# Attention with beacon keys into soft-MoE: loads spread over all partitions, the start and the pair loop reordered

## The chip, the cores and the metric

One NeuronCore of a Trainium2 chip runs the whole program. The metric is the device time of one execution in microseconds (us), the median of several runs. The engines are TensorE (PE; its weight loads are PEld), VectorE (DVE), ScalarE (ACT), GpSimd (POOL) and SyncE (SP), which only issues transfers; 16 DMA engines move the data.

## The reference

```python
# q, k, v: (8, 8, 576, 64) = (B, H, S, D); beacon_k, beacon_v: (8, 8, 16, 64); float32
scores = q @ concat(beacon_k, k).T / 8        # 592 keys; causal over the 576, the 16 beacons always seen
x = softmax(scores) @ concat(beacon_v, v)     # -> (4608, 512) tokens
logits = x @ phi                              # 32 slots, 4 per expert, 8 experts
slot_input = softmax(logits, over tokens).T @ x
slot_out[e] = relu(slot_input[e] @ w1[e]) @ w2[e]     # w1: (8, 512, 1024), w2: (8, 1024, 512)
out = softmax(logits, over slots) @ slot_out  # (4608, 512) float32
```

## The kernel before, in words

Everything is ordered by hand: the program runs under a manual schedule, so each engine takes its instructions in the order in which the code emits them, and a tile pool with a number of buffers decides when a new tile must wait for the readers of an old one. PSUM is full: two score tiles of two banks (`ps_sc`, tag sc), one A.V tile of two banks (`ps_av`, tag av), and two single banks (`ps_tr`, tag tr) for transposes and small sums.

**Loads.** SP issues k, q and v (float32, 28.3 MB) by half batches (`load_qk`, four buffers each for k and q) and batches (`load_v`, two buffers; its last 80 rows by `load_vr`). A v tile holds token 4p+t at partition p, shifted so that the 16 beacon rows fill partitions 0 to 3: `load_v` fills all partitions for b > 0 and the beacon rows are laid over partitions 0 to 3 afterwards by `load_bv` (L381), so each of these loads has to wait for the v load of the same tile; for b = 0 it loads partitions 4 to 115 and 116 to 127 (L371). The beacon keys of all heads come in one load over 64 partitions (L669). POOL issues the expert weights (33.5 MB float32, cast to float16 on the way) in 32 pieces of 512 KB (`load_weights`, L448 and L453): one in each pair but the first of a batch, two a pair in the last two batches, and what is left behind the loop. Experts 0 to 4 have room of their own; 5 takes the v buffers (`wv`), 6 and 7 the k and q buffers (`wt`), once these are free. The order of the last six pieces is w2 of experts 5, 6, 7, first halves and then second halves.

**Start** (L699 to L742). PE runs `fill` matmuls (work whose result nobody reads), turns k and q of the first half batch (`transposes`), turns the beacon keys (L710, copied to `bkA` by DVE and from there into `kTs` by POOL, `beacon_keys`), and computes the scores of pairs 0 and 1 with fills between them.

**Pair loop** (L746 to L783), 30 turns, n = 2 to 31; a pair is two heads, four pairs are one batch b. `scores(n, bank)` makes four banks of transposed scores (L514), each followed by an exp on ACT (L519) into `expT` and a causal mask on POOL (`select`, L505). `attend(n-1, hh)` multiplies the probabilities of the pair before by v (L535), `normalize` divides (DVE, L549), `x_transposes(n-3)` turns x (L561), `transposes` turns k or q two half batches ahead (L483, evicted by DVE, L495). One pair is emitted as: scores 0, scores 1, transposes, A.V of head 0, scores 2, x's turn, A.V of head 1, normalize, scores 3. The extras of a batch are put behind this: `dispatch(b-2)` (slot sums) in the first pair, `logits(b-1)` in the third, `combine_T(b-1)` and `perm_v(b+1)` in the fourth. `perm_v` turns the casted v into token order by 16 selecting matmuls into one score tile and both tr banks, and ACT (L407) and DVE (L410) copy it to `vhs`.

**Tail.** The last pair's A.V, logits and slot sums; `first` (relu of slot inputs by w1, L816), `turn`, `second` (by w2, L831); `row_sums(bb)` (L663) make the combine weights' sums for the four quarters of the output, two quarters in a PSUM bank beside the expert output `so`, the other two before and behind `second(1)`. The expert output is scaled (L863), the row factors are inverted (`row_factors`, L841 and L843), and 36 output tiles follow: a matmul (L911), an eviction by ACT or DVE in turn (L916, L918), and 13 stores (L922). `judge` tests on DVE that no sum left the range that the fast path allows; POOL prepares these tests (L884 to L888).

Of the kernel before, what the change touches and what calls it, by code (L numbers as in the profile page):

```python
# [268 lines left out]
def kernel(  # L269
# [39 lines left out]
    bkA = const.tile([P, Nb, B * H], BF, name="bkA")  # L309
# [45 lines left out]
    def load_v(b):  # L355

        t = st["v", b] = stv.tile([P, H, 4, D], FP, name="vstag", tag="v", bufs=2)
        st["r", b] = stv.tile([P, H, D], FP, name="vrem", tag="r", bufs=2)
        if b:
            lo = (b * H * S - Nb) * D
            nc.sync.dma_start(
                out=t[:, :, :, :].rearrange("p h t d -> p h (t d)"),
                in_=v.rearrange("b h s d -> (b h s d)")[lo:lo + H * S * D].rearrange(
                    "(h e) -> h e", h=H)[:, 0:4 * P * D].rearrange("h (p e) -> p h e", p=P))
        else:
            for p0, p1 in ((4, 116), (116, 128)):  # L370
                nc.sync.dma_start(  # L371
                    out=t[p0:p1, :, :, :].rearrange("p h t d -> p h (t d)"),
                    in_=v[b, :, 4 * p0 - Nb:4 * p1 - Nb, :].rearrange(
                        "h (p t) d -> p h (t d)", t=4))
# [4 lines left out]

    def load_bv(b):  # L380
        nc.sync.dma_start(out=st["v", b][0:4, :, :, :].rearrange("p h t d -> p h (t d)"),  # L381
                          in_=beacon_v[b].rearrange("h (p t) d -> p h (t d)", t=4))

    def cast_v(b, c):
# [3 lines left out]
        if c < 2:  # L388
            for hs in (slice(4 * c, 4 * c + 2), slice(4 * c + 2, 4 * c + 4)):
                nc.gpsimd.tensor_copy(  # L390
                    out=st["c", b][:, :, hs, :].rearrange("p t h d -> p h t d"),
                    in_=st["v", b][:, hs, :, :])
        else:
            nc.gpsimd.tensor_copy(out=vhs[b % 2][0:80, 4, :, 0:D], in_=st["r", b][0:80, :, :])

    def perm_v(b):

        ps = ps_sc.tile([P, 2, 512], FP, name="vps", tag="sc")
# [3 lines left out]
        for t in range(4):  # L402
            for c in range(4):
                nc.tensor.matmul(outs[c], sel[32 * c:32 * c + 32, t, :],  # L404
                                 vc[32 * c:32 * c + 32, t, :, :].rearrange("p h d -> p (h d)"),
                                 start=(t == 0), stop=(t == 3))
        nc.scalar.activation(vhs[b % 2][:, 0:2, :, 0:D],  # L407
# [9 lines left out]
    wchunks += [(e, 1, j) for j in range(2) for e in (5, 6, 7)]  # L417
    wtail = {}
# [23 lines left out]
    def load_weights(count):  # L442
        for _ in range(count):
# [7 lines left out]
            else:  # L451
                src = moe_w2[e].rearrange("(p c) d -> p c d", c=NFC)
                nc.gpsimd.dma_start(  # L453
                    out=piece(e, m, j),
                    in_=src[:, 4 * j:4 * j + 4, :].rearrange("p c d -> p (c d)"))
# [3 lines left out]
    def beacon_keys(m):  # L459
        for hh in range(2):  # L460
            c0, c1 = (H * (m // 2) + head(2 * m + u, hh) for u in range(2))
            nc.gpsimd.tensor_copy(  # L462
                out=kTs[m % 2][64 * hh:64 * hh + 64, :, 0:Nb],
                in_=bkA[64 * hh:64 * hh + 64, :, c0:c1 + 1:c1 - c0].rearrange("p n u -> p u n"))

    def transposes(m, which):
# [6 lines left out]
        else:  # L473
            if m:
                beacon_keys(m)
            dst = kTs[m % 2][:, :, Nb:Nb + S]
        for j0, j1 in ((0, 5), (5, NJ)):
            tp = ps_tr.tile([P, j1 - j0, P], BF, name="trps", tag="tr")
# [93 lines left out]
    def logits(b, t0=0, t1=NDC):  # L572
# [12 lines left out]
        if t0 == 0:  # L585
            nc.scalar.activation(dTs[b][:, :, :, :],
                                 lp[:, :, :].unsqueeze(2).broadcast_to([P, NC5, 4, NSL]), AF.Exp)
        else:
            nc.scalar.activation(dTs[b][:, :, 0, :], lp[:, :, :], AF.Exp)
            nc.vector.tensor_copy(  # L590
                out=dTs[b][:, :, 1:4, :],
                in_=dTs[b][:, :, 0:1, :].broadcast_to([P, NC5, 3, NSL]))
# [64 lines left out]
    rsp = {}  # L657

    def row_sums(bb):
        if bb == 0:  # L660
            rsp[0] = ps_av.tile([P, 2, 512], FP, name="rsps", tag="av")
        for j in range(NJ):
            nc.tensor.matmul(rsp[0][:, 1, bb * NJ + j:bb * NJ + j + 1], row_tokens(bb, j),  # L663
                             ones32[:, :], start=True, stop=True)

    with tc.manual_schedule(engines={ET.PE, ET.DVE, ET.Activation, ET.Pool, ET.SP}):
        load_qk(0, 0, first=True)
        bkf = work.tile([P, Nb, D], FP, name="bkf", tag="x")
        nc.sync.dma_start(out=bkf[0:B * H, :, :].rearrange("p n d -> p (n d)"),  # L669
                          in_=beacon_k.rearrange("b h n d -> (b h) (n d)"))  # L670
        load_v(0)
        load_bv(0)
        load_vr(0)
        load_qk(0, 1)
        load_v(1)
        load_qk(1, 0)
        load_bv(1)
        load_vr(1)
        load_qk(1, 1)
# [6 lines left out]
        make_identity(nc, idh)  # L686
        for t in kTs:
# [8 lines left out]
        nc.gpsimd.memset(sel[:, :, :], 0.0)  # L696


        fill(10, False)  # L699
        transposes(0, 0)  # L700
        fill(2, False)
        transposes(0, 1)
        bkh = work.tile([P, Nb, D], BF, name="bkh", tag="vc", bufs=1)
        hi = bkf[0:B * H, :, :].bitcast(BF)[:, :, 1::2]
        nc.scalar.activation(bkh[0:B * H, 8:Nb, :], hi[:, 8:Nb, :], AF.Copy)
        nc.vector.tensor_copy(out=bkh[0:B * H, 0:8, :], in_=hi[:, 0:8, :])
        bkp = ps_tr.tile([P, Nb, B * H], BF, name="bkps", tag="tr")
        for i in range(Nb):
            for hh in range(2):
                nc.tensor.transpose(bkp[64 * hh:64 * hh + 64, i, :], bkh[0:B * H, i, :],  # L710
                                    idb[0:B * H, 0:B * H])
        nc.vector.tensor_copy(out=bkA[:, :, :], in_=bkp[:, :, :])  # L712
        beacon_keys(0)
        fill(5, False)
        for c in range(4):
            for t in range(4):
# [3 lines left out]
                    in_=idh[32 * c:32 * c + 32, 32 * c:32 * c + 32])  # L720

# [3 lines left out]
        for c in range(2):  # L725
            cast_v(0, c)
        for bank in range(2):
            fill(3, False)
# [4 lines left out]
        for bank in range(3):  # L733
            fill(3, False)
            scores(1, bank)
        transposes(1, 0)
        perm_v(0)
        scores(1, 3)
        transposes(1, 1)
        attend(0, 0)  # L740
# [5 lines left out]
        for n in range(2, NPAIR):  # L746
            b, g = divmod(n, NG)
            scores(n, 0)
            scores(n, 1)
            if n // 2 + 1 < 2 * B:  # L750
                transposes(n // 2 + 1, n % 2)
            attend(n - 1, 0)
            scores(n, 2)
            if n >= 3:
                x_transposes(n - 3)
            attend(n - 1, 1)
            if n >= 7 and g == 3:
                combine_T(b - 1)
            normalize(n - 1)
            scores(n, 3)  # L760
            if n == NPAIR - 1:
                x_transposes(n - 2)
            if b and g == 2:
                logits(b - 1)
            if n >= 8 and g == 0:
                dispatch(b - 2)
            if b + 1 < B and g:
                parts = ((0,), (1,), (2,))[g - 1] if b else ((0,), (1, 2))[g - 2]
                for c in parts:
                    cast_v(b + 1, c)  # L770
                if g == 3:
                    perm_v(b + 1)
            if b + 2 < B:
# [3 lines left out]
                if g == 2:  # L777
                    load_bv(b + 2)
# [18 lines left out]
        fill(1)  # L797
# [3 lines left out]
        row_sums(0)  # L801
# [35 lines left out]
        rsv = stat[:, NST:NST + 36]  # L837
        rcf = rc[:, :, :].rearrange("p a j -> p (a j)")

        def row_factors(j0, j1):  # L840
            nc.vector.tensor_scalar(out=rsv[:, j0:j1], in0=rsp[0][:, 1, j0:j1], scalar1=1e-9,  # L841
                                    scalar2=None, op0=AL.add)
# [117 lines left out]
```

## Time and profile before

| what | value |
|---|---|
| median of 3 runs (range) | 203.09 us (202.74 to 204.77) |
| the profiled execution's own time | 203.09 us |
| its span in the profile | 201.4 us |
| PE / DVE / ACT / POOL busy | 163.2 / 132.2 / 133.9 / 113.9 us |
| read from HBM, written to it | 62.69 MB, 9.44 MB |
| TensorE's granted clock, mean | 0.95 |

The profiled execution took as long as the median; 1.69 us of it lie outside of the span. All shares in the profile are of the span. A DMA share of 1 in a stretch means that packets were under way on all 16 DMA engines all the time; a little over 1 is overlap of one packet's end with the next one's start. The weight transfers are counted by the bytes that they write, which is half of what they read.

### The profile page before, as it was taken

To read this page: it belongs to the slowest core of one execution; us is meant where nothing else is said; L and a number is where in the kernel's file an instruction comes from. 1 tells how busy PE (TensorE), PEld (TensorE's weight loads), DVE (VectorE), ACT (ScalarE), POOL (GpSimd) and SP (SyncE) were. 2 spreads that over 40 slices of the span, in tenths; PEclk is the share of its full clock that TensorE was granted. 3 is DMA by queue.
4 is the path that set the end of the run, shared out by engine and by line. 5 is a ranking of instruction groups with operands and counts; after the bars stand their busy time and mean duration, and the time that the engine had idled before them with its cause. 6 is when DMAs were issued, how large, how long until landed. Compare 5 with 4: busy or idle time off the path is not lost.

```text
span 201.4 us, 7361 instructions
## 1 busy us (share of the span) xinstructions
PE 163.2 (81%) x3121; PEld 107.9 (54%) x3121; DVE 132.2 (66%) x275; ACT 133.9 (66%) x172; POOL 113.9 (57%) x263
## 2 busy tenths in 40 slices
PE   6798893889889898988988899898989997966200
PEld 2433661668567476666756667675767753522000
DVE  0352784688987888887887878878837332898300
ACT  2355784689878888889887788987895230774200
POOL 6049186469649757865965786898786000890000
PEclk9999999799999999999999999999999999995855
DMA  6999999999999999999999999999999991499991
GB/s 206 254 244 365 278 361 317 270 370 311 267 271 378 264 261 349 292 275 305 356 232 279 379 273 268 264 219 217 211 216 212 213 202 30 176 410 417 408 405 78
DMA packets 29701, 55.90 MB, mean 278 GB/s; under 512 B 7228, under 2 KB 15644, under 8 KB 29660
## 3 DMA queue, kind: packets, MB, share of 16 engines
q1 hardware_dynamic: 24764, 37.98, 55.4%
q0 software_dynamic: 4608, 16.78, 41.7%
q10 hardware_dynamic: 288, 0.59, 1.0%
q8 instruction: 26, 0.43, 0.8%
q14 instruction: 15, 0.12, 0.2%
HBM read 62.69 MB, written 9.44 MB: 358 GB/s over the span
## 4 chain that ended last, share of the span: by engine, by line
PE 60%; DMA 10%; ACT 9%; DVE 8%; POOL 3%; issue 3%; SPq 0%; ACTq 0%; DVEq 0%; POOLq 0%
PE sc L514 15%; PE av L535 15%; PE trps L483 9%; DMA wt<-in_moe_w_dram 7%; ACT expT L519 5%; PE xtps L561 5%; DVE osb L918 4%; ACT vh L407 4%; PE vpt L404 2%; DMA kstag<-in_k_dram 2%; PE fill L655 2%; PE fps L911 2%; PE lgps L580 2%; PE vps L404 2%; PE sips L619 2%
## 5 line engine op out<-in xcount | busy, mean ns | idle before, releaser
L519 ACT ACTIVATE expT<-sc 128x992 f16<-128x992 f32 (+3 forms) x128 | 104.8, 867 | 20.6 <-PE sc L514 20.0
L505 POOL TENSOR_SCALAR_AFFINE_SELECT expT<-expT 128x224 f16<-128x224 f16 (+3 forms) x128 | 54.9, 439 | 40.1 <-ACT expT L519 39.2
L514 PE MATMUL sc<-qT,kT 64*128 64x80 bf16 (+4 forms) x576 | 43.8, 246 | 10.8 <-ACT expT L519 5.5
L535 PE MATMUL av<-vh,expT 128*128 128x65 f16 (+1 forms) x960 | 40.4, 195 | 0.4 <-DVE x L549 0.2
L535 PEld LDWEIGHTS <-expT 128*128 128x128 f16 (+1 forms) x960 | 33.7, 98 | 4.5 <-POOL expT L505 0.6
L495 DVE COPY kT<-trps 128x640 bf16<-128x640 bf16 (+1 forms) x31 | 22.7, 773 | 19.8 <-PE trps L483 19.3
L514 PEld LDWEIGHTS <-kT 64*128 64x128 bf16 x576 | 17.0, 95 | 28.1 <-issue 22.2
L495 DVE COPY qT<-trps 128x640 bf16<-128x640 bf16 (+1 forms) x30 | 22.0, 774 | 8.2 <-PE trps L483 6.3
L549 DVE TENSOR_TENSOR x<-av,r 128x640 f16<-128x640 f32 x32 | 26.4, 825 | 1.1
L390 POOL CAST vc<-vstag 128x512 f16<-128x512 f32 x32 | 18.6, 611 | 1.8 <-DMA vstag<-in_beacon_v_dram 1.8
L916 ACT ACTIVATE osb<-fps,rc 128x512 f32<-128x512 f32 (+1 forms) x18 | 11.0, 678 | 12.2 <-PE fps L911 10.9
L568 DVE COPY xT<-xtps 128x576 f16<-128x576 f16 x31 | 14.2, 457 | 6.5 <-PE xtps L561 6.5
L561 PE MATMUL xtps<-idh,x 128*128 128x128 f16 (+2 forms) x160 | 14.1, 216 | 1.1 <-issue 1.0
L918 DVE TENSOR_SCALAR osb<-fps,rc 128x512 f32<-128x512 f32 (+1 forms) x19 | 12.8, 731 | 1.3 <-PE fps L911 1.1
L655 PE MATMUL fill<-eT,onesh 128*128 128x512 f16 x35 | 11.4, 453 | 1.7 <-POOL onesh L684 1.5
L407 ACT ACTIVATE vh<-vps 128x1024 f16<-128x1024 f32 x8 | 8.2, 1027 | 6.6 <-PE vpt L404 6.6
L561 PEld LDWEIGHTS <-x 128*128 128x128 f16 (+2 forms) x160 | 9.0, 97 | 6.6 <-issue 6.0
L410 DVE CAST vh<-vpt 128x512 f16<-128x512 f32 x16 | 10.3, 685 | 3.4 <-PE vpt L404 3.4
L911 PE MATMUL fps<-so,eT 128*128 128x512 f16 (+1 forms) x37 | 11.6, 433 | 0.5 <-DVE stat L841 0.3
L462 POOL COPY kT<-bkA 64x32 bf16<-64x32 bf16 x32 | 7.4, 231 | 7.9 <-DVE bkA L712 6.9
L483 PE MATMUL trps<-idb,kstag 128*64 128x128 bf16 x270 | 11.6, 234 | 0.1
L483 PE MATMUL trps<-idb,qstag 128*64 128x128 bf16 x270 | 10.7, 222 | 0.5 <-DVE vh L410 0.4
(98 smaller groups left out, 186.7 us busy)
## 6 DMA issues: line engine op xcount, KB each, us to landing
kstag<-in_k_dram SPq DMA_DIRECT2D x15, 576.0 KB, 9.4
qstag<-in_q_dram SPq DMA_DIRECT2D x15, 576.0 KB, 13.4
out_dram<-osb SPq DMA_DIRECT2D x11, 768.0 KB, 7.6
vstag<-in_v_dram SPq DMA_DIRECT2D x7, 1024.0 KB, 15.3
w1h<-in_moe_w_dram POOLq DMA_DIRECT2D x10, 512.0 KB, 8.6
w2h<-in_moe_w_dram POOLq DMA_DIRECT2D x10, 512.0 KB, 8.5
wt<-in_moe_w_dram POOLq DMA_DIRECT2D x8, 512.0 KB, 12.2
wv<-in_moe_w_dram POOLq DMA_DIRECT2D x4, 512.0 KB, 11.6
```

What stands on the lines that cost most here:

```text
L390: nc.gpsimd.tensor_copy(out=st["c", b][:, :, hs, :].rearrange("p t h d -> p h t d"), in_=st["v", b][:, hs, :, :])
L407: nc.scalar.activation(vhs[b % 2][:, 0:2, :, 0:D], ps[:, :, :].rearrange("p c (h d) -> p c h d", d=D), AF.Copy)
L483: nc.tensor.transpose(tp[lo:hi, j - j0, :], t[:, hh, j, :].bitcast(BF)[:, 1::2], idb[:, :])
L495: nc.vector.tensor_copy(out=do, in_=ti)
L505: nc.gpsimd.affine_select(out=ap, in_=ap, compare_op=AL.is_ge, fill=0.0, base=cbase, pattern=pat, channel_multiplier=-1)
L514: nc.tensor.matmul(sc[:, hh, col:col + qw], kTs[n // 2 % 2][po:po + D, n % 2, c * P:(c + 1) * P], qTs[n // 2][po:po + D, n % 2, q0:q0 + qw ...
L519: nc.scalar.activation(ex[:, :, base:base + w], sc[:, :, 0:w], AF.Exp, scale=scale)
L535: nc.tensor.matmul(av[:, i, :], exps[n % 2][0:KW[c], hh, o:o + P], vhs[b % 2][0:KW[c], c, h, :], start=(c == 0), stop=(c == i))
L549: nc.vector.tensor_tensor(out=xs[b][:, :, head(n, 0):head(n, 1) + 1:head(n, 1) - head(n, 0), :].rearrange("p i h d -> p h i d"), in0=av[:, ...
L561: nc.tensor.transpose(tp[:, QLO[i]:QLO[i] + QW[i]], xs[b][0:QW[i], i, 2 * t:2 * t + 2, :].rearrange("p h d -> p (h d)"), idh[0:QW[i], 0:QW ...
L911: nc.tensor.matmul(f[:, 0:hw], row_tokens(bb, j), so1[:, hw * i:hw * i + hw], start=True, stop=True)
L918: nc.vector.tensor_scalar(out=ou, in0=f[:, 0:hw], scalar1=rc[:, bb, j:j + 1], scalar2=None, op0=AL.mult)
```

## The change

It touches the loads, the start, the order within a pair and the order behind the weights.

- **Loads.** The v load of batch 0 goes over all 128 partitions for heads 1 to 7, as for the other batches; head 0 comes in two loads (partitions 4 to 63, 64 to 127). `load_bv` is gone. The beacon values come with token n at partition n: batch 0's in a load of its own over 16 partitions, all batches' in one load over 128 partitions (`bvf`, 512 KB in pieces of 256 bytes), and `perm_v` adds them by one more matmul, while the rows of `sel` for partitions 0 to 3 are zero. The beacon keys are loaded over 128 partitions. The order on SP is k and q (1, 0) before v (1).
- **Start.** q's turn of the first half batch uses the two banks of the A.V tile. The beacon keys go straight from PSUM to `kTs` by DVE. `sel` is built first. Ten of the fill matmuls are dropped, `perm_v(0)` moves up into pair 1 and uses the A.V tile, and two of the v casts go to DVE.
- **Pair.** All four score banks move ahead of the A.V half that they stood behind, x's turn stands behind the first A.V half, and each batch's extras are one a pair: `perm_v(b)` between scores 0 and 1 of the first pair, `dispatch` in the second, `logits` in the third, `combine_T` in the fourth. The exp of the logits writes one copy, and DVE makes the other three.
- **Tail.** The last weight piece is issued in two halves. `row_sums(0)` and `(1)` have PSUM tiles and factors of their own; `row_sums(2)` and `(3)` are put among the output tiles of quarters 0 and 1, and POOL's test of the sums into `judge`.

```diff
     def load_v(b):
-        if b: ... one load over 128 partitions
-        else:
-            for p0, p1 in ((4, 116), (116, 128)): ... all heads
+        h0 = 0 if b else 1
+        ... one load over 128 partitions of heads h0 to 7
+        if b == 0:
+            nc.gpsimd.memset(t[0:4, 0, :, :], 0.0)
+            for p0, p1 in ((4, 64), (64, 128)): ... head 0
-    def load_bv(b):
-        nc.sync.dma_start(out=st["v", b][0:4, :, :, :].rearrange("p h t d -> p h (t d)"),
-                          in_=beacon_v[b].rearrange("h (p t) d -> p h (t d)", t=4))
     def perm_v(b):
-        ps = ps_sc.tile([P, 2, 512], FP, name="vps", tag="sc")
+        pool, tag = (ps_sc, "sc") if b else (ps_av, "av")
+        ps = pool.tile([P, 2, 512], FP, name="vps", tag=tag)
...
+            if t == 0:
+                lhsT, rhs = (idh[:, b::B], bvh) if b else (idh[0:Nb, 0:Nb], bvh[0:Nb])
+                nc.tensor.matmul(outs[0][0:Nb, :], lhsT, rhs..., start=False, stop=False)
     def load_weights(count):
-                nc.gpsimd.dma_start(out=piece(e, m, j), in_=... 4 columns c)
+                cs = 2 if (e, m, j) == WLAST else 4
+                for c in range(0, 4, cs): ... one load for cs columns
     def logits(b, t0=0, t1=NDC):
-        if t0 == 0:
-            nc.scalar.activation(dTs[b][:, :, :, :],
-                                 lp[:, :, :].unsqueeze(2).broadcast_to([P, NC5, 4, NSL]), AF.Exp)
-        else: ... (as below)
+        nc.scalar.activation(dTs[b][:, :, 0, :], lp[:, :, :], AF.Exp)
+        nc.vector.tensor_copy(out=dTs[b][:, :, 1:4, :],
+            in_=dTs[b][:, :, 0:1, :].broadcast_to([P, NC5, 3, NSL]))
     the pair loop
             scores(n, 0)
+            if b and g == 0:
+                perm_v(b)
             scores(n, 1)
             if n // 2 + 1 < 2 * B:
                 transposes(n // 2 + 1, n % 2)
+            scores(n, 2)
             attend(n - 1, 0)
-            scores(n, 2)
             if n >= 3:
                 x_transposes(n - 3)
+            scores(n, 3)
             attend(n - 1, 1)
-            if n >= 7 and g == 3:
-                combine_T(b - 1)
             normalize(n - 1)
-            scores(n, 3)
+            if b > 1 and g == 1:
+                dispatch(b - 2)
             if b and g == 2:
                 logits(b - 1)
-            if n >= 8 and g == 0:
-                dispatch(b - 2)
+            if b and g == 3:
+                combine_T(b - 1)
...
-                if g == 3:
-                    perm_v(b + 1)
     the tail
-        row_sums(2)
         second(1)
         nc.vector.tensor_scalar(out=so1[:, :], in0=so, scalar1=rd[:, 0:1], ...)
-        row_sums(3)
-        row_factors(2 * NJ, 4 * NJ)
...
                 nc.sync.dma_start(out=outr[bb, :, j0:j1, :], in_=osb[:, 0:j1 - j0, :])
+                if bb in (0, 1) and j0 == 3:
+                    row_sums(bb + 2, ps_g.tile([P, NJ], FP, name="rsps", tag="g"))
```

## The prediction

> **What bounds the kernel now.** I read the DMA rows of the page first, because the kernel reads 62.69 MB.
>
> ```profile
> PEclk9999999799999999999999999999999999995855
> DMA  6999999999999999999999999999999991499991
> GB/s 206 254 244 365 278 361 317 270 370 311 267 271 378 264 261 349 292 275 305 356 232 279 379 273 268 264 219 217 211 216 212 213 202 30 176 410 417 408 405 78
> ```
>
> The 16 DMA engines are full from the second slice to slice 33 (about 166 us), pause for the end of the MLP, and are full again with the stores. Slices with more weights show fewer GB/s, as weights count by what they write: 213 GB/s of weights alone are 426 GB/s read.
>
> The end of the chain of waits says what the pause waits for (start us, us, what).
>
> ```profile
> 154.15 14.88 DMA wt<-in_moe_w_dram
> 169.08 1.04 PE rsps L831 x13
> 170.15 0.76 DVE so L863
> 170.95 0.66 PE rsps L663 x9
> 171.86 0.61 PE fps L911 x3
> ```
>
> The last weight piece lands just before 169.08. Then come the last 16 matmuls of `second`, the scaling, two quarters' row sums, and the first output matmul. But TensorE is nearly late too: in the list of waits this one is only 0.6 us long. So two paths end together at 169: the transfers, and the computing (start, pair loop, MLP). A change must shorten both.
>
> Then I cut the time into stretches, for the DMA share and the rate (last two columns; before them busy us of PE, PEld, DVE, ACT, POOL and the granted clock).
>
> ```profile
> 5.00:13.00 8.00, 6.89 (x87) 3.39 (x85) 4.50 (x20) 2.75 (x4) 0.50 (x2) 1.00 1.16 219
> 13.00:20.00 7.00, 6.23 (x64) 2.48 (x67) 1.46 (x2) 5.09 (x7) 6.16 (x14) 1.00 1.06 364
> 20.00:24.00 4.00, 3.49 (x81) 2.35 (x75) 2.59 (x6) 2.55 (x4) 0.33 (x1) 1.00 0.92 266
> 30.00:36.00 6.00, 2.84 (x44) 1.52 (x46) 2.53 (x6) 3.10 (x5) 3.70 (x8) 0.87 1.09 309
> 86.87:103.57 16.70, 15.58 (x350) 11.26 (x350) 13.96 (x29) 14.46 (x19) 12.09 (x29) 1.00 1.06 301
> 162.00:164.00 2.00, 2.00 (x33) 1.19 (x29) 0.69 (x1) 0.82 (x2) 0.00 (x0) 1.00 1.08 217
> 164.00:166.00 2.00, 2.00 (x34) 1.15 (x36) 0.70 (x2) 0.38 (x1) 0.00 (x0) 1.00 0.92 184
> 166.00:168.00 2.00, 2.00 (x41) 1.15 (x33) 0.44 (x1) 0.00 (x0) 0.00 (x0) 1.00 0.40 82
> ```
>
> Three places waste DMA time. From 5 to 13 us the engines are full (1.16) and move 219 GB/s; the same kind of float32 loads moves 364 right after. From 20 to 24 they are partly empty. From 164 on they run dry one after the other.
>
> SyncE's own waits, and two of the computing engines', complete the picture (total us, times, longest; the third line is of 34.76 to 138.42 us).
>
> ```profile
> SPq L381 <- DMA vstag<-in_v_dram: 39.2, 7, 6.6
> PE sc L514 <- ACT expT L519: 5.5, 10, 0.6
> ACT expT L519 <- PE sc L514: 14.7, 42, 1.5
> ```
>
> The beacon load (L381) overwrites part of the tile that the v load is filling, so SyncE stands, seven times, until v has landed; after the first of these (to 21.05 us) the engines have run empty. In the loop ScalarE is the computing engine nearest to its limit (14.46 of the 16.70 us of a batch) and waits 14.7 us over six batches for scores.
>
> **The transfers, term by term.** What counts is when the last weight piece lands, 168.7 us by its last packet in the trace.
>
> *Loads over all partitions.* In 5 to 13 us lie the beacon keys (64 partitions), batch 0's v (112 and 12), its beacons (4) and its remainder (80). The trace's packet records show the v packets of 1 KB at 65 to 96 ns there and at 46 to 53 in all later v loads, which cover 128 partitions. 219 GB/s for 8 us is 1.75 MB; at 364 GB/s that is 4.8 us. So the most to be won is 3.2 us, the least nothing (if the slowness belongs to the first use and not to the shape). I take 2.6: 896 of the 1020 v packets get the good shape, head 0 and the remainder do not.
>
> *The wait at L381.* 20 to 24 us at 266 GB/s in place of the 349 that I read for 24 to 28 loses 0.95 us. The wait goes with `load_bv`; I take 0.7 off (0 to 1.0). The other six waits cost nothing today, since the share stays at 1.05 or more: weights fill the engines meanwhile.
>
> *Short pieces.* Beacon values now come in 128 + 1024 pieces of 256 bytes. The trace has 5120 such packets (v's remainder): 18 ns median, 24 mean, about 50 in the bad stretch. 1152 x 18 to 24 / 16 engines = 1.3 to 1.7 us: I add 1.5, bounds 0.9 (13 ns, phi's 128-byte packets) and 3.6. They lie in the saturated stretch, so nothing hides them. The Trainium skill (DMA: Bandwidth & Descriptors, "Specifications") asks for 512 bytes at least for the full rate, and so speaks against this part. By it a piece costs no less than one of 512 bytes, an estimate of 23 ns from half of the 1 KB row, 1.7 us in all, and the sum below would be -3.2; the median of 18 ns shows a little less than that.
>
> *Uneven finish.* After 164 us 184, 82 and (168 to 170) 4 GB/s for 2 us each are 0.54 MB; at 217 GB/s all engines would be done at 166.5, 2.2 us before the last one is. Something loads a few engines more than the rest; the eight beacon loads of 4 partitions, 32 packets each, are the only regular small ones. I take 1.6 off, bounds 0 and 2.2. The same page ("Why a DMA increments its semaphore by 16 and not by 1") says that a load takes as many engines as divide its slowest dimension, the lowest-numbered ones: 4 partitions, 4 engines. By it each of these gets an estimated 8 x 8 packets of about 50 ns, 3.2 us, more than the others, which would explain the whole 2.2, and the sum would be -4.0.
>
> Sum: -2.6 - 0.7 + 1.5 - 1.6 = -3.4; the last piece lands at about 165.3.
>
> **The computing.** It must be ready by then, 3.0 us before today's 168.3 (end of the matmuls that needed no wait). *Start:* `bkA` and POOL's copies stand between the beacon turn and the scores (10.41 to 11.73 us); two DVE copies, for which POOL's 0.23 us is the nearest row, save some 0.5. Three fills of 0.75 us between pair 1's scores go, 2.2. `sel`'s 1.96 us on DVE move to where DVE is idle until 7.06. Together -2.5 (bounds 0, -3.2). *Row sums:* `row_sums(2)`, 0.7 us of PE, leaves the place ahead of `second(1)`. That is 3.2, just enough with no gain in the loop at all. *Loop:* with a score bank ahead of each A.V half ScalarE finds work sooner; dT's exp falls from 0.70 to 0.30 us (the rows at L586 and L589), DVE gets 0.31 more (row at L590), PE one 512-column matmul of 0.22 a batch. VectorE with 13.96 + 0.3 and ScalarE with 14.1 are the floors of a batch, 16.70 to 17.97 now. `normalize` of a batch's first pair needs the x buffer that `dispatch` now reads behind it: DVE stands some 0.5 us there, and the turns' evictions behind it wait, about 0.5 once a batch. I take 1 us a batch as won, 7 in all; bounds +11 (first rival) and -20 (both floors reached). It hides whole under the weights: a faster loop frees buffers sooner, but the engines that would use them are full. So PE will stand idle for several us ahead of the last pieces.
>
> **Behind the last piece.** Only half of it remains to be multiplied, 8 matmuls for 16: -0.5 of the 1.04, but the extra landing takes 0.1: -0.4. The next chain row, 170.95 to 171.86, is `row_sums(3)` and what follows: -0.9. Among the output tiles both row sums cost PE 2 x 0.7 and DVE 2 x 0.45 us; the stores run at 409 GB/s with six buffers and PE is busy 9.6 of 22 us, so this is hidden; uncovered it would be 2.3. POOL's test of the sums (1.13 + 1.12 + 0.94) falls into the output as before. *Clock:* the one dip in the loop follows the idle PE of 30 to 36 us (clock 0.87, half speed for 3.4 us in the clock records). Idle ahead of the last weights, PE would do the last matmuls and the first output tiles at half speed: +0.4, bounds 0 and 0.9.
>
> **Total:** -3.4 - 0.4 - 0.9 + 0.4 = -4.3 on the execution's 203.09 us (span 201.4 to 197.1). The median is the same execution's: 198.8.
>
> **Rivals.**
> *The loop gets slower (209.3).* PE takes its work in order; A.V now stands behind score banks whose PSUM tile an exp must free. Ten such waits of 0.55 us stand in the profile; one in each of 30 pairs is 20 more, 11 us. The computing path ends 11 - 3.2 later than 168.3; less the 0.7 that it waits today and the 0.9 of the row sums that is +6.2. It decides from 4.8 us of loss on, 0.16 a pair. Against it: ScalarE is the one that waits (14.7 us); for it: POOL's masks and casts (12.09 of 16.70) get less time before A.V needs them.
> *The first loads stay slow (201.4).* Then the 2.6 fall away. For it: the first microseconds also hold instruction loads; against it: the kq loads of 2 to 5 us run at full speed.
> *More comes out (196.3).* All lower bounds: -3.2 - 1.0 + 0.9 - 2.2 - 0.4 - 0.9 + 0 = -6.8. For it: the rates after and before these stretches.
> *It does not do what it says:* the loop is faster and the transfers do not move, as the short pieces take what the shape gives (0 - 0.7 + 3.6 - 1.6 - 0.9 = +0.4; the -0.4 and +0.4 of the end cancel): 203.5.
>
> **How the numbers follow.** Forecast 0.53, more comes out 0.17, first loads stay slow 0.14, short pieces eat it 0.07, slower loop 0.09. The range 195.8 to 202.4 holds the first three cases with their spread, 0.83. A measurement tells about 1% from no change: below 201.06 lie the forecast, "more" and a part of the third case, 0.76; above 205.1 the slower loop, with a little more 0.10; between, 0.14.
>
> **What would show it.** Right: 5 to 13 us above 300 GB/s; no SyncE wait on v; the last `wt` piece lands at 165 +- 1 and PE waits for it for several us; the output starts 4 us sooner and lasts as long. Wrong: a landing near 168, or a computing path that ends last (no wait for `wt` in the chain), or stores below 400 GB/s because row sums hold the evictions up.

## The result, and the profile after

The changed kernel takes **211.32 us** (median of 4 runs, 210.44 to 212.66) beside 203.93 us for the kernel before in the same session (4 runs): a ratio of **1.037, 95% interval 1.031 to 1.042**. It is slower by 7.4 us. The forecast was 198.8 us, with a range that ended at 202.4. The profiled execution took 212.66 us with a span of 210.9; before it was 203.09 and 201.4. Here and below a median is of all runs of a kernel, a ratio compares its faster runs with those of the kernel before in the same session, and where a profile is of one of the slower runs (experiments 2, 4 and 6) it is read for rows and pair lengths alone.

The strip of slices of the page after (40 slices of 5.27 us):

```profile
PEclk9999966999999699969997999999999999997855
DMA  6999999999999999999999999399999990399991
GB/s 217 325 385 307 325 320 269 345 331 258 302 368 260 250 365 285 260 256 353 264 263 304 302 196 177 61 207 187 199 213 214 214 204 13 139 414 416 403 396 46
```

Three things differ from before. The second slice already moves 325 GB/s (254 before). The clock shows dips in slices 14, 18 and 22, in the middle of the pair loop. And slices 24 to 26 fall to 196, 177 and 61 GB/s: the DMA engines have too little to do there.

The same by stretches (busy us of PE, PEld, DVE, ACT, POOL, then the clock, the DMA share, GB/s):

```profile
5.00:13.00 8.00, 6.49 (x73) 3.41 (x72) 5.41 (x16) 3.49 (x5) 2.54 (x5) 1.00 1.09 343
13.00:20.00 7.00, 6.24 (x114) 3.54 (x112) 3.92 (x7) 6.10 (x9) 3.87 (x9) 1.00 1.09 359
20.00:24.00 4.00, 3.84 (x88) 2.75 (x87) 3.41 (x6) 3.94 (x6) 2.69 (x8) 1.00 1.12 274
124.00:128.00 4.00, 3.04 (x58) 1.96 (x57) 3.02 (x7) 3.14 (x4) 3.35 (x9) 1.00 0.85 148
128.00:132.00 4.00, 3.36 (x57) 1.80 (x57) 2.52 (x4) 2.24 (x3) 0.97 (x3) 1.00 0.95 165
132.00:136.00 4.00, 3.82 (x88) 2.79 (x85) 3.40 (x8) 3.56 (x5) 3.19 (x8) 1.00 0.23 23
```

The start is what was wanted: 343 GB/s from 5 to 13 us where 219 stood. The pair loop begins at 19.5 us instead of 23.3 (first score matmul of pair 2). It ends late: the last pair's first score matmul is at 159.5 us instead of 149.3. So the loop itself lost 14 us, and with it go the weights, which the loop issues. That is why the engines are only partly full from 124 to 132 us and nearly empty from 132 to 136 (share 0.23): the last load of k or q was issued at 115.5 us, and from 119.4 to 133.7 the loop issues only four weight pieces.

The loop's loss can be located by the length of a pair. This table (and the one behind the experiments) is worked out from the trace: from the first score matmul of one pair to that of the next, mean over batches 2 to 7 (for the fourth pair 2 to 6).

| kernel | 1st pair | 2nd | 3rd | 4th | batch |
|---|---|---|---|---|---|
| before | 4.59 | 3.22 | 4.36 | 4.91 | 17.08 |
| after | 7.19 | 4.05 | 3.99 | 4.09 | 19.32 |

The first pair holds `perm_v` now, and it pays far more than the fourth pair, which held it before, wins. The list of waits of the kernel after has a line that before does not have at all, the first of these (us in total, times, longest):

```profile
PE vpt L401 <- DVE eT L653: 5.0, 6, 0.8
ACT vh L408 <- PE vpt L401: 13.9, 7, 4.1
PE sc L527 <- ACT expT L532: 5.6, 17, 1.0
```

The third line is the wait that the slower rival of the prediction was built on, a score bank that an exp must free: 5.6 us in all, as before (5.5). It did not grow. The first is a new one: the matmuls of the v turn wait six times, 0.8 us each, for `combine_T`'s copy of `eT`. The timeline of one such pair shows how it comes about (start, duration, engine, line, operation; in brackets the idle time before it and what ended it):

```profile
66.50 0.31 PE L650 MATMUL etps<-idh,dT 128*128 128x128 f16 x3
66.74 0.38 PE L527 MATMUL sc<-qT,kT 64*128 64x496 bf16 x2
67.04 0.82 DVE L562 TENSOR_TENSOR x<-av,r 128x640 f16<-128x640 f32 x1
67.07 0.39 PE L401 MATMUL vpt<-vc,sel 32*128 32x512 f16 x1
67.23 1.00 ACT L532 ACTIVATE expT<-sc 128x992 f16<-128x992 f32 x1 [1.18 <-PE sc L527]
67.78 0.45 DVE L653 COPY eT<-etps 128x576 f16<-128x576 f16 x1
68.28 0.37 PE L401 MATMUL vpt<-vc,sel 32*128 32x512 f16 x1 [0.83 <-DVE eT L653]
70.25 1.03 ACT L408 ACTIVATE vh<-vps 128x1024 f16<-128x1024 f32 x1 [2.02 <-PE vpt L401]
```

`combine_T` turns its weights into a tr bank (66.50) and DVE must copy it out. But `combine_T` stands behind `normalize` now, so DVE first does normalize's 0.82 us operation and copies `eT` only from 67.78 to 68.23. `perm_v` needs both tr banks. TensorE, which takes its instructions in the order of the code, stands for 0.83 us in the middle of the turn, with all of the next scores behind it, and ScalarE idles 2.02 us: its next instruction is the copy of the finished turn, and the exps behind that need the scores.

The end is as planned, but 9 us later: no row sums lie between the scaling of `so` and the first output matmul (0.05 us instead of 0.95).

```profile
180.10 0.75 DVE L869 TENSOR_SCALAR so<-so,rd 128x512 f16<-128x512 f32 x1 [2.03 <-PE so L847]
180.90 1.46 PE L918 MATMUL fps<-so,eT 128*128 128x256 f16 x7 [0.86 <-DVE so L869]
```

### The profile page after: what moved, and what is told of

It is laid out like the page before. It is cut to its first block, busy times and chain, and to the rows that moved or that the text cites. A ratio compares the mean times of both kernels' runs of the same rounds, so it can differ in the third digit from the quotient of the medians.

```text
span 210.9 us, 7342 instructions
## 1 busy us (share of the span) xinstructions
PE 167.0 (79%) x3101; PEld 110.9 (53%) x3101; DVE 137.4 (65%) x291; ACT 132.4 (63%) x171; POOL 118.4 (56%) x263
## 4 chain that ended last, share of the span: by engine, by line
## 5 line engine op out<-in xcount | busy, mean ns | idle before, releaser
L518 POOL TENSOR_SCALAR_AFFINE_SELECT expT<-expT 128x224 f16<-128x224 f16 (+3 forms) x128 | 55.6, 442 | 48.8 <-ACT expT L532 46.2
L548 PE MATMUL av<-vh,expT 128*128 128x65 f16 (+1 forms) x960 | 41.7, 197 | 0.7 <-issue 0.6
L527 PEld LDWEIGHTS <-kT 64*128 64x128 bf16 x576 | 18.9, 96 | 24.0 <-issue 15.0
L386 POOL CAST vc<-vstag 128x512 f16<-128x512 f32 x30 | 17.7, 619 | 5.8 <-DVE kT L467 5.8
L496 PE MATMUL trps<-idb,kstag 128*64 128x128 bf16 x270 | 14.6, 251 | 4.2 <-DVE vh L411 3.2
L401 PE MATMUL vpt<-vc,sel 32*128 32x512 f16 x64 | 13.2, 425 | 5.0 <-DVE eT L653 5.0
L496 PEld LDWEIGHTS <-kstag 128*64 128x64 bf16 x270 | 11.4, 126 | 8.9 <-issue 8.5
L559 DVE TENSOR_SCALAR stat<-av 128x10 f32<-128x10 f32 x32 | 5.4, 169 | 13.2 <-PE av L548 13.2
L401 PE MATMUL vps<-vc,sel 32*128 32x512 f16 x64 | 11.0, 426 | 2.6 <-POOL vc L386 2.6
L918 PE MATMUL fps<-so,eT 128*128 128x512 f16 (+1 forms) x37 | 10.9, 419 | 1.2 <-DVE so L869 0.9
(104 smaller groups left out, 198.8 us busy)
## 6 DMA issues: line engine op xcount, KB each, us to landing
wt<-in_moe_w_dram POOLq DMA_DIRECT2D x7, 512.0 KB, 10.5
```

The source lines that it names most:

```text
L386: (nc.vector if c == 1 and b == 0 else nc.gpsimd).tensor_copy(out=st["c", b][:, :, hs, :].rearrange("p t h d -> p h t d"), in_=st["v", b][ ...
L401: nc.tensor.matmul(outs[c], sel[32 * c:32 * c + 32, t, :], vc[32 * c:32 * c + 32, t, :, :].rearrange("p h d -> p (h d)"), start=(t == 0), ...
L496: nc.tensor.transpose(tp[lo:hi, j - j0, :], t[:, hh, j, :].bitcast(BF)[:, 1::2], idb[:, :])
L518: nc.gpsimd.affine_select(out=ap, in_=ap, compare_op=AL.is_ge, fill=0.0, base=cbase, pattern=pat, channel_multiplier=-1)
L527: nc.tensor.matmul(sc[:, hh, col:col + qw], kTs[n // 2 % 2][po:po + D, n % 2, c * P:(c + 1) * P], qTs[n // 2][po:po + D, n % 2, q0:q0 + qw ...
L548: nc.tensor.matmul(av[:, i, :], exps[n % 2][0:KW[c], hh, o:o + P], vhs[b % 2][0:KW[c], c, h, :], start=(c == 0), stop=(c == i))
```

## The experiments

First I suspected the new place of `perm_v` itself (theory P), the order of score banks and A.V halves (O), or the loads and the tail (D).

**1. `perm_v` back.** The kernel after, with one move:

```diff
-            if b and g == 0:
-                perm_v(b)              # between scores 0 and 1 of the first pair
...
+                if g == 3:
+                    perm_v(b + 1)      # behind the casts of the fourth pair
```

> Only perm_v goes back to the end of the fourth pair; the new bank order, the new places of the other extras, loads, start and tail stay. Theory P (perm_v between scores 0 and scores 1 of a batch's first pair is what slows the loop): the first pairs fall from 7.2 to about 4.1 us, the fourth rise from 4.1 to about 5.5, the loop gets 10 to 14 us shorter, and the time comes to 198 to 201 us. Rival O (A.V standing behind score banks is what slows it): the time stays above 207 us.

Measured: 215.99 us, ratio 1.059 (1.046 to 1.071). It is no better, by the ratio worse, and the loss went along: the fourth pair now takes 7.03 us, and the wait for `eT` is 6.9 us in six times. P falls.

**2. The whole old pair loop in the kernel after.** The order of `scores`, `attend`, `normalize` and all four extras as before the change; loads, start and tail stay new.

> The whole pair loop in the order of before (bank order, places of all extras), everything else of the change kept. Both P and O: the loop is as long as before (about 130 us) and starts 3.9 us sooner, so 198 to 200 us, which is what the prediction's terms of the transfers gave. Third theory D (the new loads or the new tail cost time of their own): above 203 us.

Measured: 204.06 us, 0.992 (0.986 to 0.998); a batch takes 17.61 us. So the pair loop is nearly the whole loss; but the new loads, start and tail bring only 0.8%, 1.7 us, of the 4 us that they should, and the batch is still 0.53 us longer than before (experiment 8).

**3. The kernel before, with `perm_v` alone moved.**

> The kernel before, with perm_v alone moved behind scores 0 of the next batch's first pair. P: each of seven batches gets about 2.3 us longer, the time rises by 10 to 16 us to 213 to 219 us. O: no change within 1%, 201 to 205 us.

Measured: 203.77 us, 0.997 (0.993 to 1.001), a batch of 17.30 us: no change. The new place of `perm_v` is harmless by itself.

**4. The kernel after, with the old order of banks and A.V halves alone** (`attend(0)`, scores 2, x's turn, `attend(1)`, `normalize`, scores 3).

> The changed kernel with the old order of banks and A.V halves inside a pair; perm_v and the other extras stay at their new places. P: first pairs stay near 7 us, time 208 to 213 us. O: the loop recovers, time below 202 us.

Measured: 207.39 us, 1.014 (1.004 to 1.024). A part of it, about 2% by the ratios. Scores 3 stand between `normalize` and `combine_T` here, and the wait for `eT` is only 1.2 us in five times.

That pointed to `combine_T` (theory X), against the order of the banks (O).

**5. One line in the kernel after:** `combine_T` ahead of `normalize`, as before the change.

```diff
             attend(n - 1, 1)
+            if b and g == 3:
+                combine_T(b - 1)
             normalize(n - 1)
...
-            if b and g == 3:
-                combine_T(b - 1)
```

> The kernel after, with one line moved: combine_T is emitted ahead of normalize again (as before the change), so that its copy on DVE no longer stands behind normalize's 0.82 us operation. Theory X (the extras' new places): in the trace of the changed kernel the second bank of the v turn (vpt, L401) waits for DVE's copy eT six times, 0.8 us each, and the transposes and the scores behind it are late by as much; some 0.8 us a batch over seven batches come back, 5 us, so 205 to 207 us; PE's wait for eT is gone from the waits. Theory O (A.V behind score banks): this wait is not what holds the loop, 210 to 212 us.

Measured: **203.76 us**, 0.996 (0.992 to 1.0005). The whole loss in time is gone with one line moved, more than theory X had. (The loop itself is not yet as short as before: a batch takes 18.06 us beside 17.08. The earlier start and the tail make up for that.) The timeline of the same pair:

```profile
64.58 0.46 DVE L653 COPY eT<-etps 128x576 f16<-128x576 f16 x1 [1.14 <-PE etps L650]
64.80 0.67 PE L401 MATMUL vpt<-vc,sel 32*128 32x512 f16 x2
65.40 0.82 DVE L562 TENSOR_TENSOR x<-av,r 128x640 f16<-128x640 f32 x1
66.59 1.03 ACT L408 ACTIVATE vh<-vps 128x1024 f16<-128x1024 f32 x1 [0.63 <-PE vpt L401]
```

The copy comes first, both halves of the turn start at once, the copy of `vh` 1.8 us after the turn's start instead of 3.2. The first pair goes from 7.19 to 5.76 us, that is by 1.43, while the wait was 0.83. Most of the rest is the clock. In the profiled execution of the kernel after the clock falls to half in three of these pairs; here are the three stretches of the kernel after, and behind them the loop of this experiment:

```profile
69.14:72.55 3.41, 3.11 (x38) 1.51 (x30) 2.03 (x4) 1.86 (x2) 0.38 (x2) 0.50 1.05 251
89.62:93.03 3.41, 3.26 (x50) 2.59 (x49) 2.29 (x5) 2.04 (x3) 1.56 (x4) 0.50 1.06 238
110.10:113.51 3.41, 3.34 (x50) 2.60 (x49) 2.29 (x5) 1.96 (x3) 1.64 (x4) 0.50 1.09 273
```

```profile
60.00:160.00 100.00, 88.92 (x1954) 63.72 (x1951) 76.89 (x159) 76.55 (x98) 70.26 (x155) 1.00 1.06 267
```

The three first pairs with a dip (batches 3, 4 and 5) take 7.52, 7.75 and 7.79 us, the three without 6.68 to 6.71. So of the sum, 6 x 0.92 = 5.5 us are the wait with what stands behind it, and 0.84 + 1.07 + 1.11 = 3.0 us come from the dips. That the wait brings the dips on is inferred, and it does not always do so: in the loops with this wait at 0.8 us or more there are three such dips here, two in experiment 6, one in 11 and none in 1. Between 45 and 150 us there is none in the kernel before and in experiments 2 to 5, 7 to 9 and 12; experiment 10, whose stalls are of another kind, has three again. The three dips here begin 20.48 us apart, six times their length of 3.41, and in the 3.41 us ahead of each TensorE is busy for 2.17, 2.22 and 2.14 us. Cut into such stretches, experiment 5's loop has none under 2.4 us from 30 to 150 us. So whether a stall costs a dip seems to hang on how it falls into these stretches; but that is not all, as one stretch of 2.12 us here (from 127.17) and two of 2.11 and 2.10 in experiment 1 (from 106.32 and 123.39) have no dip behind them.

**6 and 7. The parts alone on the kernel before:** all three extras at their new places; then only the order of the banks.

> The kernel before, with only the extras at their new places: dispatch in the second pair, logits in the third, combine_T behind normalize and scores 3 in the fourth; order of the banks, perm_v, loads, start and tail as before. Theory X (the places of the extras make the loop slow): of the 7.4 us that the changed kernel is slower, the order of the banks was worth 3.9 when it was taken back, so the places should be worth the other 3.5 and more, since the new loads and start save 3 us: 207 to 210 us, and the first pair of a batch gets shorter by less than the second gets longer. Theory I (interaction: each move is harmless in the old surroundings and costs only together with the others): 203 to 205 us, no change.

Measured: 212.85 us, 1.033 (1.024 to 1.043), more than theory X had, and the same line in the waits, 4.8 us in six times. No interaction with the rest of the change is needed.

> The kernel before, with only the order of score banks and A.V halves of the changed kernel (scores 2, A.V of head 0, x's turn, scores 3, A.V of head 1, combine_T, normalize), everything else as before. Theory O (A.V behind score banks costs by itself): what was saved by taking this order back in the changed kernel, 3.9 us, is lost here: 207 to 209 us, and the pair with perm_v at its end (the fourth) gets longer most. Theory I (interaction): 203 to 205 us; a pair without extras may even get shorter than before, as in the changed kernel (3.44 us).

Measured: 206.58 us, 1.013 (1.008 to 1.018): it costs by itself, but less than the 3.9. The fourth pair grows from 4.91 to 5.52 us. Where it sits is seen in ScalarE's rows around the v turn, of this experiment and then of the kernel before:

```profile
82.79 3.26 ACT L519 ACTIVATE expT<-sc 128x992 f16<-128x992 f32 x4
87.48 1.03 ACT L407 ACTIVATE vh<-vps 128x1024 f16<-128x1024 f32 x1 [1.43 <-PE vpt L404]
```

```profile
84.88 0.70 ACT L519 ACTIVATE expT<-sc 128x640 f16<-128x640 f32 x1 [0.61 <-PE sc L514]
85.79 1.03 ACT L407 ACTIVATE vh<-vps 128x1024 f16<-128x1024 f32 x1 [0.21 <-PE vpt L404]
```

With all four banks early, all four exps run in one go (3.26 us), and nothing is left for ScalarE to do while TensorE works on the extras: it idles 1.43 us ahead of the copy. Before, the last bank's exp (84.88) lay beside the turn, and the idle times were 0.61 and 0.21 us. The wait of the turn for `eT` is there too, though `combine_T` stands ahead of `normalize`: 1.4 us in six times, where the kernel before has none. How the 2.6 us divide between the two was not separated.

**8. The old pair loop, and no seventeenth matmul in the v turn** (L406) for batches 1 to 7. This kernel leaves the beacon values of these batches out of its result.

> The changed kernel with the old pair loop, and in addition without the seventeenth matmul of perm_v in batches 1 to 7 (the beacon values of these batches are left out of A.V). Theory M (the one matmul of 128 rows, L406, breaks the four-way side-by-side of the sixteen matmuls of 32 rows: the turn takes 1.77 us with it and 1.32 us before the change): 0.45 us a batch come back, 3.1 us in seven batches, 200.5 to 202 us, and the turn is 1.3 us long again. Rival T (the transfers end last by then: the last piece lands near 171): 203 to 205 us although the turn is shorter.

Measured: 201.14 us, 0.987 (0.981 to 0.993). By the ratios that is 0.5%, 0.9 us, less than experiment 2, and the two intervals overlap. A batch takes 17.09 us, as before the change, beside 17.61. The turn in experiment 2, where the sixteen matmuls run four side by side (32 rows each) and the one of 128 rows stands alone:

```profile
85.91 0.73 PE L401 MATMUL vpt<-vc,sel 32*128 32x512 f16 x2
86.57 0.40 PE L406 MATMUL vps<-bvh,idh 128*16 128x512 f16 x1
86.91 0.39 PE L401 MATMUL vps<-vc,sel 32*128 32x512 f16 x2
87.77 1.03 ACT L408 ACTIVATE vh<-vps 128x1024 f16<-128x1024 f32 x1 [0.99 <-PE vpt L401]
```

Without it (experiment 9) the second group of four starts 0.36 us behind the first, here 1.0 (0.94 in experiment 5). The whole turn, from its first matmul to the end of its last, takes 1.83 us in experiment 2 and mostly 1.38 in experiments 8 and 9, as in the kernel before: one matmul costs 0.45 us, twice the 0.22 at which the prediction had put it. It begins only when the four before it are nearly done, and the next four begin behind it; that it has to wait for all groups of rows is how I read this. In this experiment the transfers end last, as the prediction had wanted; the end of its chain and the stretches:

```profile
151.80 15.67 DMA wt<-in_moe_w_dram
168.15 0.76 DVE so L869
```

```profile
162.00:164.00 2.00, 2.00 (x36) 1.05 (x32) 0.69 (x1) 0.00 (x0) 0.00 (x0) 1.00 0.75 142
164.00:166.00 2.00, 1.36 (x23) 0.41 (x12) 0.00 (x0) 0.00 (x0) 0.00 (x0) 1.00 0.48 90
166.00:168.00 2.00, 1.10 (x13) 0.31 (x12) 0.00 (x0) 0.00 (x0) 0.00 (x0) 1.00 0.13 27
```

TensorE now waits 1.5 us for the last weights (1.36 and 1.10 us busy of 2), and the last packet lands at 167.2 us instead of 168.7. So a part of what the loop won is not seen in the time: from the first score matmul of pair 8 to that of pair 31 it takes 97.5 us here and 100.3 in experiment 2.

**9 and 10. The best version, and the weights earlier.** Experiment 9 is experiment 2 with the beacon values of batches 1 to 7 laid over the v tiles by small loads, as before the change, in place of the matmul, and without the `bvf` load, which only that matmul needs. Experiment 10 adds

```diff
-            load_weights((0, 1, 1, 1)[g] if b < 6 else 2)
+            load_weights((b > 0, 1, 1, 1)[g] if b < 6 else 2)
```

> The changed kernel with the old pair loop, and with the beacon values of batches 1 to 7 laid over the v tiles by small loads as before the change, in place of the seventeenth matmul; loads of batch 0, start and tail stay changed. Theory M (the 128-row matmul inside the v turn is the whole difference between the old pair loop here and there): as fast as without the beacon values, 200.5 to 202 us, and the turn is 1.3 us long. Theory B (the small loads behind the v loads cost what they cost before the change, as SyncE waits for v again): 203 to 205 us. The last weight piece lands near 167.5 in the first case.

Measured: **200.64 us**, 0.983 (0.979 to 0.988): faster than both kernels. Theory M holds: a batch takes 16.96 us, and the small loads that the change removed cost nothing that shows here.

> As g1, with one weight piece also in the first pair of batches 1 to 5 (five pieces are issued earlier; POOL issues them, and the number in the last two batches falls). Theory W (the transfers are paced by the pair loop, which issues one piece a pair, so the 1 MB that the first loads are ahead at 13 us is waited away by 80 to 100 us): the last piece lands 2 to 3 us sooner, and the end moves as far as the computing lets it, 198.5 to 200.5 us. Theory F (the engines are full in the loop whatever is queued, as the prediction had it): the queue only gets longer, k, q and v come later for it, and the time stays or grows, 200.5 to 203 us.

Measured: 213.91 us, 1.040 (1.033 to 1.047). Both theories miss the size. W is wrong: the last packet lands at 167.4 us, no earlier than in experiment 9 (167.3). F has the right sign. Its chain of waits says what happened:

```profile
49.17 19.99 DMA vstag<-in_v_dram
69.17 11.21 DMA vstag<-in_beacon_v_dram
80.50 1.17 POOL vc L390 x2
94.06 21.45 DMA vstag<-in_v_dram
115.53 6.76 DMA vstag<-in_beacon_v_dram
```

A v load takes 20 us from issue to landing (15 in experiment 9), the small load that must wait for it another 11, and only then can POOL cast v and TensorE turn it. Three pairs grow to 9 to 10.5 us. With the engines full, five pieces more move little more: by 120 us the weights read are 3.9 MB ahead of experiment 9, all reads together 0.8 MB, and by 160 us nothing. They push back what the loop needs next. How the earlier weights would do without the small loads was not run. The Trainium skill (DMA: Bandwidth & Descriptors, "Queues, rings and completion order") says that each engine takes packets in turn from the queues that have work, which agrees with such a delay; no run here separates it from the mere length of the queue.

**11 and 12. `combine_T` alone and `dispatch` alone on the kernel before.**

> The kernel before, with combine_T alone moved behind normalize and scores 3 of the fourth pair (perm_v of the next batch follows it, as before). Theory X (combine_T's copy on DVE, behind normalize, holds the tr bank that the v turn needs): the second vpt waits for eT as in the changed kernel, 0.8 us a batch and what follows from it; 206 to 211 us, most of the 8.9 us that the three extras' places cost together on this kernel. Theory Y (dispatch in the second pair is what cost there): 203 to 205 us.

Measured: 210.18 us, 1.029 (1.022 to 1.034), and its waits have the line again:

```profile
PE vpt L404 <- DVE eT L644: 4.8, 6, 0.8
```

Its fourth pair takes 5.67 us in each of batches 1 to 6, where these take 4.74 to 5.17 in the kernel before, 4.88 in the mean: 6 x 0.79 = 4.7 us of the 5.8 that arrive at the end.

> The kernel before, with dispatch alone moved from the first to the second pair. Theory Y (the second pair gets 1.3 us longer and the first only 0.3 shorter): 1 us a batch, 6 batches, 208 to 210 us. Theory X (combine_T's place is the cause): 203 to 205.5 us.

Measured: 203.69 us, 1.000 (0.996 to 1.0035): nothing. The second pair is 1.3 us longer and the first 0.8 shorter, the third 0.5.

| kernel | 1st pair | 2nd | 3rd | 4th | batch | ratio |
|---|---|---|---|---|---|---|
| 1 after, perm_v back | 4.06 | 4.08 | 3.99 | 7.03 | 19.16 | 1.059 |
| 2 after, old pair loop | 4.75 | 3.17 | 4.28 | 5.41 | 17.61 | 0.992 |
| 3 before, perm_v moved | 6.45 | 3.10 | 4.27 | 3.48 | 17.30 | 0.997 |
| 4 after, old bank order | 6.19 | 4.53 | 4.16 | 3.89 | 18.77 | 1.014 |
| 5 after, combine_T first | 5.76 | 4.11 | 4.06 | 4.13 | 18.06 | 0.996 |
| 6 before, extras moved | 4.26 | 4.55 | 3.86 | 5.76 | 18.43 | 1.033 |
| 7 before, bank order | 4.48 | 3.54 | 3.95 | 5.52 | 17.49 | 1.013 |
| 8 as 2, no 17th matmul | 4.62 | 3.11 | 4.33 | 5.03 | 17.09 | 0.987 |
| 9 as 2, old beacon loads | 4.62 | 3.10 | 4.32 | 4.92 | 16.96 | 0.983 |
| 10 as 9, weights earlier | 4.57 | 3.07 | 5.28 | 6.81 | 19.73 | 1.040 |
| 11 before, combine_T behind | 4.80 | 3.08 | 4.27 | 5.67 | 17.82 | 1.029 |
| 12 before, dispatch moved | 3.83 | 4.53 | 3.86 | 4.94 | 17.16 | 1.000 |

## Why the prediction was wrong, point by point

**The step that failed is the loop term,** "I take 1 us a batch as won, 7 in all ... It hides whole under the weights". The loop lost 14 us, more than the bound of +11. From the first score matmul of pair 8 to that of pair 31 the kernel before takes 97.6 us, the kernel after 111.8, experiment 5 104.2, experiment 2 100.3 and experiment 8 97.5. Three things were in it:

- *`combine_T` behind `normalize`* was not costed at all. The prediction listed the extras' new places, looked at `dispatch` and the x buffer (0.5 us, and `dispatch` costs nothing: experiment 12), and did not follow the tr banks that `combine_T` fills and `perm_v` needs. Taking it back gives 7.6 us (experiment 5), some 3 of them from the dips of the clock, and adding it alone to the kernel before costs 5.8 (experiment 11). It is no more than a copy of 0.45 us that stands behind an operation of 0.82.
- *The seventeenth matmul* was put at 0.22 us a batch by its columns; it makes the turn 0.45 us longer, and 2.8 us of the loop go with it (experiments 2 and 8), of which 0.9 to 1.7 us are seen in the time by the ratios (2 against 8 and 9).
- *A score bank ahead of each A.V half* was to give ScalarE work sooner. It does, and, as I read the rows of experiment 7, takes it away from where the extras stand; by itself it costs 2.6 us there. Together with the new places of the other extras it makes up the 3.9 us between the loops of experiments 5 and 2.

**The slower rival** had the sign and, by chance, nearly the time (209.3), with 0.09. Its mechanism was not what happened: the waits of scores for exps stayed at 5.6 us. The order of the banks that it blamed does cost something by itself, but along another path (experiment 7).

**What was right.** *Loads over all partitions:* 343 GB/s in place of 219. By 13 us the kernel after had read 3.75 MB, before 2.74 (packet records, weights by what they read). 1.01 MB at the 364 GB/s of the loads that follow is 2.8 us; the term was 2.6. *Start:* scores begin 0.95 us and the loop 3.8 us sooner (-2.5 was the term, -3.2 its bound). *Row sums:* the 0.95 us between scaling and output are 0.05, as said; the output phase is 29.0 us instead of 28.2, though (first store issued at 181.93, span 210.9), so most of that gain is spent among the stores.

**What experiments 8 and 9 show of the transfers,** since there the loop is about as short as before. The last packet lands at 167.2 and 167.3 us: -1.5 in place of -3.4. The lead of the first loads was kept in experiment 8 (0.88 MB at 13 us, 0.98 at 160).

*The wait at L381* (-0.7) and *the short pieces* (+1.5) fall into the same stretch. SyncE no longer waits for v in the kernel after, but from 20 to 24 us it moves 274 GB/s, not the 349 that the term counted on, although the engines are full there (share 1.12). Experiment 8 is alike; experiment 9 has the wait back and does without `bvf`. Their rows, experiment 8 first:

```profile
20.00:24.00 4.00, 3.53 (x82) 2.46 (x80) 3.28 (x6) 3.81 (x5) 2.77 (x8) 1.00 1.18 261
```

```profile
20.00:24.00 4.00, 3.36 (x70) 2.20 (x69) 3.61 (x8) 3.81 (x6) 2.37 (x7) 1.00 1.06 308
```

By the packet records the 256-byte packets from 13 to 24 us take 2.85 us of all 16 engines in experiment 8 (1664 packets) and 0.80 us in experiment 9 (640). So the 1024 pieces of `bvf` (256 KB, not the 512 KB given with the change) cost about 2.0 us of the engines' time: they cost what the term said, and more. The lead over the kernel before stays at 0.88 and 0.87 MB (at 13 and 24 us, experiment 8), so they seem to have used up what the missing wait gave. By 40 us experiments 8 and 9 are level (13.07 and 13.00 MB).

*The uneven finish* (-1.6, "the eight beacon loads of 4 partitions") is the term of the transfers that failed: the change removes these loads, and in experiment 8 the engines still run dry one after the other. 142, 90 and 27 GB/s for 2 us each are 0.52 MB, as much as the 0.54 before, and the last packet lands some 2.7 us behind an even finish (2.2 before), an estimate at the 213 GB/s of weights alone. Experiment 9, which has seven of these loads back, finishes more evenly: 164 and 46 GB/s for 2 us each from 164 us on, which is some 1.3 us by the same estimate. So the rule that the prediction weighed there (the Trainium skill, DMA: Bandwidth & Descriptors, "Why a DMA increments its semaphore by 16 and not by 1") does not explain it here; what does stays open.

*"The engines that would use them are full"* was right: experiment 10 could not move the landing. But full is no cushion for a slow loop: when the loop in the kernel after fell behind, the pieces were issued late, and the last packet came at 175.9 us.

**The clock.** +0.4 for a dip behind an idle TensorE was put at the end of the kernel only. In the kernel after, dips came in the middle of the loop, for 3.0 us. The dip that was forecast is seen in experiment 8, where TensorE does wait for the last weights: half speed from 168.53 us for 3.41 us, and the first seven output matmuls take 2.72 us instead of 1.46 in experiment 9.

Put together by the ratios: loads, start and tail with the old loop and the old beacon values, without `bvf`, bring -1.7% (experiment 9), the seventeenth matmul +0.8 (2 against 9), the other moves in the loop +0.5 (5 against 2), and `combine_T`'s place +4.0 (after against 5): +3.7%. The third figure is within its uncertainty of nothing and the second only just outside. In the loop the other moves cost 3.9 us (104.2 against 100.3), so something makes up for most of that in experiment 5. A part is seen ahead of pair 8: from pair 2 to pair 8 experiment 5 takes 27.3 us and experiment 8 29.9, of which a longer early dip of the clock (6.83 us at half speed instead of 3.41) can be up to 1.7. The rest was not separated.

## What to carry to other kernels

When an instruction is moved, list the buffers that it holds and who asks for them next, on the engine that empties them: a copy of 0.45 us put behind an operation of 0.82 us cost 7.6 us here, the dips of the clock included, since the bank that it empties was one that TensorE needed in the middle of a sequence. Look also at what stands beside the extras: when ScalarE had all of its exps behind it, the extras on TensorE left it idle (experiment 7). And where the DMA engines were full, issuing earlier only reordered (experiment 10): ask whose load comes later for it.

## What the hardware showed that was not expected

- A matmul of 128 rows between groups of four 32-row matmuls made their sequence 0.45 us longer, not 0.22: 1.83 us in experiment 2, 1.38 in experiments 8 and 9.
- The clock can fall to half for 3.41 us in the middle of a busy loop: TensorE is busy for 3.11 to 3.34 us of the three stretches at 0.50, and the idle time lies ahead of them (busy for 2.14 to 2.22 of the 3.41 us just before).
- Five 1 MB loads issued earlier on one queue stretched two v loads on another to 20.0 and 21.5 us from issue to landing (15.2 in experiment 9), with hardly a change of the total: 62.05 MB read by 165 us beside 62.21.
- A load of 256 KB in pieces of 256 bytes took about 2.0 us of all 16 engines' time in a full stretch (experiments 8 and 9).
